# Row loads by head parity, 64x64 transposes, and V of the first batch on a second DMA queue

## The chip, the cores and the metric

One core of one Trainium2 chip. The metric is device time in microseconds (us), the median of several runs. Fast runs of one kernel mostly agree within about 0.6%. PE is the matmul engine, DVE the vector engine, ACT the engine for activations, POOL and SP the engines that here mostly issue DMAs. The profile books every DMA of this program, from whichever queue, on the same 16 DMA engines. A packet here is one contiguous run of a transfer; its bytes are those that land, so a load that rounds f32 to bf16 counts at half of what it reads.

## The reference, cut to what matters

```python
# q, k, v: (8 batches, 8 heads, 576 tokens, 64), float32
scores = q @ k^T / 8 - slope[h] * |i - j|,  masked to 0 <= i - j < 128
attn   = softmax(scores)
x      = (attn @ v) as (8 * 576 tokens, 512)
h      = x @ w_in                       # 512 -> 2048
out    = (h * cos(h)) @ w_out           # 2048 -> 512
```

Almost all the work is in the two last products. Attention of batch c+1 is interleaved with the products of the 512-token chunk c. The first batch has nothing to hide behind.

## The kernel before: the parts that matter

The kernel collects operations with the tiles that they read and write, orders them with a small list scheduler, and emits them with semaphores. POOL's operations keep the order of the program text.

```python
def load_qk(which, src, b, pl):          # batches 0 and 1: rows on partitions
    fns = []
    for g in range(2):                   # two DMAs of 64 partitions, f32 -> bf16 on the way
        fns.append(... qB[which][64*g:64*g+64, 2*pl:2*pl+2, :] <- heads 4g+2pl, 4g+2pl+1 ...)
    op("pool", fns, ...)

def load_v(b, order=range(NBLK)):        # five tiles of 128 (the last 64) tokens x 8 heads x 64
    for t in order:                      # f32 -> bf16 on the way: packets of 64 elements
        op("pool", [vp[b%2][0:rows, t, :, 0:64] <- v[b, :, 128*t:..., :]], ...)

def load_w_in(u): ...                    # 4 loads on POOL's queue, packets of 512 elements

# ---- order of the program (POOL keeps it) ----
for pl in range(2):
    load_qk("q", q, 0, pl); load_qk("k", k, 0, pl)
    if pl == 0:
        constants()                      # masks' input, identity: on POOL
load_v(0)
masks()                                  # 8 exponentials of 128x512 on ACT
... transposes of q and k of batch 0 (PE, 18 of 128x128 per half) ...
for u in range(4): load_w_in(u)
... q, k of batch 1; w_out; V of batch 1 ...
attention(0)
```

P*V of the first half of the tokens needs V tiles 0 and 1, that of the second half tiles 1 to 3, that of the last 64 tokens tiles 3 and 4.

The softmax here doesn't subtract the row's maximum and nothing guards it: scores larger than these inputs give would overflow.

## Time and profile before

| | before |
|---|---|
| time, median of 5 runs | 330.28 us (329.52 to 330.59) |
| first scores / first P*V / first P*V of the last 64 tokens ("tail") / first output matmul | 10.69 / 15.01 / 29.63 / 43.29 us |
| last k of batch 0 landed | 12.32 us |

From the page of the profile: the span, the engines' busy times, PE's busy tenths in 40 slices of the span, the clock row, and the chain of work that ended last, by engine.

```profile
span 328.4 us, 6317 instructions
PE 311.0 (95%) x2504; PEld 161.5 (49%) x2544; DVE 197.9 (60%) x440; ACT 212.6 (65%) x313; POOL 101.3 (31%) x133
...
PE   2589999999999999999999999999999999999995
...
PEclk9999999999999999999999999999999999999999
...
PE 89%; DVE 3%; ACT 2%; POOL 2%; issue 2%; DMA 1%; POOLq 0%; ACTq 0%
```

PE is the limit everywhere except in the first two or three slices of 8.2 us. A change to the first batch's loads can move only that stretch. The clock row does not show what the matmuls' durations show: up to about 24 us PE runs at half rate (128x256 matmuls start 0.21 us apart, later 0.11). The trace's clock records begin with full rate at 24.2 us, and the row shows full rate before the first record as well.

The chain of waits of the first 30 us, its part just before the first P*V (start, duration, what):

```profile
5.83 1.17 POOL qrows L311 x2
7.00 0.54 POOL krows L311
7.54 4.78 DMA krows<-in_k_dram
...
12.36 1.19 PE ps L419 x17
...
13.58 0.82 DVE kt L431
14.40 0.48 DVE p L515
...
15.01 0.32 PE ps L550 x3
```

The second pair of row loads is issued only at 5.83 us, after POOL has built the constants. Its k is waited for until 12.32. Then come its transposes, its eviction on DVE, the first masking behind it in DVE's order, and P*V.

How V and w_in reach the core in this stretch (DMA view, 8 to 16 us; the last column is the median time from issue to landing):

```profile
w_inb<-in_moe_w_in_dram POOLq DMA_DIRECT2D x4, 512.0 KB, 9.5
vp<-in_v_dram POOLq DMA_DIRECT2D x4, 128.0 KB, 5.2
```

What two queues do to each other, while an output store on SP's queue met loads on POOL's (DMA view, 52.5 to 53 us):

```profile
q1 hardware_dynamic: 78, 0.16, 93.3%
q0 software_dynamic: 83, 0.01, 31.7%
```

78 store packets of 2 KB and 83 load packets of 128 B started in that half microsecond. That is nearly one to one, equal turns, although one packet was sixteen times the other.

### The profile page before, as it was taken

What the parts mean: (1) busy time and instruction counts of PE and PEld (TensorE: products, weight loads), DVE (VectorE), ACT (ScalarE), POOL (GpSimd) and SP (SyncE); (2) the same over time, 40 slices, a digit from 0 to 9 for tenths busy, and PEclk for the clock granted to TensorE, in tenths of its full rate; (3) what the DMA queues carried; (4) which work ended last, traced back from release to release, by engine and by line L of the source; (5) the groups of instructions that cost most, each with busy time, mean ns of one, the idle gap of its engine ahead of it and who ended that gap; (6) DMA issues with size and microseconds to landing.
All of it is one profiled execution on the core that took longest, in us unless ns stands there. A gap on an engine that the chain in (4) does not pass through costs nothing.

```text
span 328.4 us, 6317 instructions
## 1 busy us (share of the span) xinstructions
PE 311.0 (95%) x2504; PEld 161.5 (49%) x2544; DVE 197.9 (60%) x440; ACT 212.6 (65%) x313; POOL 101.3 (31%) x133
## 2 busy tenths in 40 slices
PE   2589999999999999999999999999999999999995
PEld 2367755444544454445444644554455444444442
DVE  2569858585848683969586867576567361254000
ACT  5669768686868585867785788669767663263211
POOL 8999530194572726800780050000000000000000
PEclk9999999999999999999999999999999999999999
DMA  6999999999999999991999395100010000201112
GB/s 89 160 206 204 207 157 177 156 150 151 183 158 153 208 115 162 171 92 52 156 168 105 72 152 39 66 33 2 32 64 2 34 1 32 93 5 64 66 67 93
DMA packets 133918, 35.29 MB, mean 107 GB/s; under 512 B 123136, under 2 KB 129280, under 8 KB 133888
## 3 DMA queue, kind: packets, MB, share of 16 engines
q0 software_dynamic: 100288, 18.36, 70.7%
q1 hardware_dynamic: 33600, 16.52, 21.9%
q8 instruction: 20, 0.33, 0.4%
q14 instruction: 10, 0.08, 0.1%
HBM read 36.70 MB, written 9.44 MB: 141 GB/s over the span
## 4 chain that ended last, share of the span: by engine, by line
PE 89%; DVE 3%; ACT 2%; POOL 2%; issue 2%; DMA 1%; POOLq 0%; ACTq 0%
PE ps L688 37%; PE ps L642 33%; PE ps L665 5%; PE ps L470 5%; PE ps L550 3%; PE ps L614 2%; PE ps L553 2%; DMA krows<-in_k_dram 1%; PE ps L419 1%; DVE p L515 1%; ACT p L500 1%; PE ps L460 1%; POOL qrows L311 1%; PE ps L536 1%; PE ps L538 1%
## 5 line engine op out<-in xcount | busy, mean ns | idle before, releaser
L688 PE MATMUL ps<-w_outb,gT 128*128 128x512 bf16 x548 | 133.4, 379 | 1.9 <-issue 0.6
L642 PE MATMUL ps<-xT,w_inb 128*128 128x512 bf16 x500 | 117.9, 379 | 1.2 <-DVE gT L651 0.4
L651 DVE TENSOR_TENSOR gT<-ps,cos 128x512 bf16<-128x512 f32 x128 | 81.8, 686 | 46.8 <-PE ps L688 29.0
L647 ACT ACTIVATE cos<-ps,halfpi 128x512 f32<-128x512 f32 x128 | 81.8, 689 | 23.0 <-PE ps L688 11.9
L688 PEld LDWEIGHTS ps<-w_outb,gT 128*128 128x128 bf16 x576 | 53.6, 98 | 57.9 <-issue 2.2
L500 ACT ACTIVATE p<-ps 128x768 bf16<-128x768 f32 (+1 forms) x64 | 56.1, 915 | 29.3 <-PE ps L470 29.2
L642 PEld LDWEIGHTS ps<-xT,w_inb 128*128 128x128 bf16 x512 | 46.8, 98 | 55.8 <-DVE gT L651 4.8
L320 POOL DMA_DIRECT2D vp<-in_v_dram x40 | 34.0, 907 | 54.2 <-PE ps L553 46.9
L515 DVE TENSOR_TENSOR p<-p,emask 128x768 bf16<-128x768 bf16 (+1 forms) x64 | 39.1, 613 | 0.2
L694 ACT ACTIVATE ob<-ps 128x512 f32<-128x512 f32 x24 | 14.3, 597 | 33.8 <-PE ps L688 33.8
L330 POOL DMA_DIRECT2D qnat<-in_q_dram x30 | 25.5, 920 | 30.9 <-DMA qt<-qnat 30.9
L330 POOL DMA_DIRECT2D knat<-in_k_dram x30 | 25.6, 926 | 5.4 <-DMA kt<-knat 5.0
L584 DVE TENSOR_TENSOR xnat<-ps,rec 128x256 bf16<-128x256 f32 x64 | 26.6, 418 | 0.7
L628 ACT ACTIVATE xT<-ps 128x256 bf16<-128x256 bf16 (+3 forms) x41 | 14.5, 355 | 18.0 <-PE ps L614 17.9
L550 PE MATMUL ps<-vp,p 128*128 128x65 bf16 x256 | 23.0, 199 | 1.6 <-DVE p L515 1.6
L550 PEld LDWEIGHTS ps<-vp,p 128*128 128x128 bf16 x256 | 17.5, 100 | 11.2 <-issue 4.2
L553 PE MATMUL ps<-vp,p 128*128 128x65 bf16 x192 | 20.7, 197 | 0.0
L470 PE MATMUL ps<-qt,kt 64*128 64x128 bf16 (+1 forms) x320 | 20.6, 253 | 0.0
L696 DVE COPY ob<-ps 128x512 f32<-128x512 f32 x12 | 8.3, 690 | 18.4 <-PE ps L688 18.0
L614 PE MATMUL ps<-ident,xnat 128*128 128x128 bf16 x128 | 18.4, 227 | 0.5 <-DVE xnat L584 0.5
L582 DVE RECIPROCAL rec<-ps 128x4 f32<-128x4 f32 x64 | 11.5, 180 | 11.5 <-PE ps L553 10.4
L665 PE MATMUL ps<-xT,w_inb 128*128 128x256 bf16 x128 | 17.4, 281 | 0.7 <-ACT ptail L492 0.5
(52 smaller groups left out, 201.9 us busy)
## 6 DMA issues: line engine op xcount, KB each, us to landing
out_dram<-ob SPq DMA_DIRECT2D x36, 256.0 KB, 2.0
vp<-in_v_dram POOLq DMA_DIRECT2D x32, 128.0 KB, 8.2
qnat<-in_q_dram POOLq DMA_DIRECT2D x24, 128.0 KB, 6.0
knat<-in_k_dram POOLq DMA_DIRECT2D x24, 128.0 KB, 5.8
w_inb<-in_moe_w_in_dram POOLq DMA_DIRECT2D x4, 512.0 KB, 9.5
w_outb<-in_moe_w_out_dram POOLq DMA_DIRECT2D x4, 512.0 KB, 17.8
qrows<-in_q_dram POOLq DMA_DIRECT2D x8, 144.0 KB, 7.4
krows<-in_k_dram POOLq DMA_DIRECT2D x8, 144.0 KB, 8.2
```

The costliest lines, as they stand in the source:

```text
L320: op("pool", [lambda e, t=t, rows=rows: e.dma_start(vp[b % 2][0:rows, t, :, 0:64], v[b, :, 128 * t:128 * t + rows, :].rearrange("h p d -> ...
L330: fns.append(lambda e, t=t, rows=rows: e.dma_start(nat[which][0:rows, t, :, :], src[b, :, 128 * t:128 * t + rows, :].rearrange("h p d -> p ...
L470: ins = e.matmul(ps[:, banks[x], c0:c1], keys_ap(b, x, pr, kc), query_ap(b, x, pr, qb, 128 * nb), start=True, stop=True)
L500: op("act", lambda e: e.activation(P[i][:, :, lo:512], src_[:, :, lo:512], ACTF.Exp, scale=0.125), w=held + [("P", i)], occ=920 if u[1] el ...
L515: op("dve", lambda e: e.tensor_tensor(P[i][:, :, lo:512], P[i][:, :, lo:512], EM[:, 2 * pr:2 * pr + 2, lo:512], ALU.mult), r=[("P", i), (" ...
L550: ins = e.matmul(o, P[i][:, x, d0:d0 + 128], V[:, kc, h, 0:65], start=True, stop=not two)
L553: ins = e.matmul(o, P[i][:, x, p0:p0 + 128], V[:, kc - 1, h, 0:65], start=False, stop=True)
L642: op("pe", lambda e, kc=kc: e.matmul(ps[:, bank, :], w_in[:, kc, 128 * fc:128 * fc + 128], xT[:, kc, r0:r0 + CH], start=(kc == 0), stop=(k ...
L647: op("act", lambda e: e.activation(cosb[ci][:, :], ps[:, bank, :], ACTF.Sin, bias=halfpi[:, 0:1]), r=["halfpi"], w=[("B", bank), ("cos", c ...
L651: op("dve", lambda e: e.tensor_tensor(gT[gi][:, fc, :], ps[:, bank, :], cosb[ci][:, :], ALU.mult), r=[("cos", ci)], w=[("B", bank), ("g", ...
L665: op("pe", lambda e, i=i, fc=fc, kc=kc: e.matmul(ps[:, bank, 256 * i:256 * i + 256], w_in[:, kc, 128 * fc:128 * fc + 128], xT[:, kc, r0:r0 ...
L688: op("pe", lambda e, t=t, fc=fc, bank=bank: e.matmul(ps[:, bank, :], gT[gi][:, fc, 128 * t:128 * t + 128], w_out[:, fc, :], start=(fc == 0 ...
```

## The change

The intent: bring q and k in with one DMA per two head pairs and all four loads before the constants; halve the mask exponentials; transpose in 64x64 tiles that fit the new layout; and free POOL's queue of V of batch 0 by sending it, unrounded, over SP's queue, so that w_in can follow k at once on POOL's. POOL then rounds V to bf16.

```diff
 def load_qk(which, src, b, pl):
-    two DMAs of 64 partitions, heads 4g+2pl, 4g+2pl+1
+    op("pool", [lambda e: e.dma_start(
+        qB[which][:, 2 * pl:2 * pl + 2, :],
+        src[b, 4 * pl:4 * pl + 4, :, :].rearrange("(k x) (s j) d -> (x s) k (j d)", x=2, j=9))], ...)
+
+def load_v0():                           # vst lies in gT[1], which is still free
+    for t in range(NBLK):
+        op("sp", [lambda e, t=t, rows=rows: e.dma_start(vst[0:rows, t, :]..., v[0, :, 128*t:..., :]...)],
+           r=[("qB", "k", 0 if t < 2 else 1)], w=[("vst", t)], ...)   # waits for k to land
+def round_v0():
+    for t in range(NBLK):
+        op("pool", tensor_copy vp[0][0:rows, t, :, 0:64] <- vst, r=[("vst", t), ...], w=[("v", 0, t)], ...)
 ...
 masks:  8 exponentials of 128x512 on ACT  ->  8 of 128x256, and 4 copies on DVE
 transposes: 18 of 128x128  ->  36 of 64x64 per half
 units of batch 0: pairs 0, 2, 1, 3  ->  0, 1, 2, 3
 scheduler: one DMA wire in its model  ->  one per issuing engine
 ...
 for pl in range(2):
     load_qk("q", q, 0, pl)
     load_qk("k", k, 0, pl)
-    if pl == 0:
-        constants()
-load_v(0)
+constants()                              # identity first
+load_v0()
 masks()
 ...
 for u in range(4):
     load_w_in(u)
+round_v0()
```

More of the change, by code (lines that the diff above doesn't have):

```diff
@@ L89, in schedule @@
         free = {e: 0 for e in ENG}
-        wire = self.WIRE0
+        wire = {e: self.WIRE0 for e in ENG}
         mode, table = 0, None
@@ L140, in schedule @@
             if o.dma is not None:
-                wire = max(wire, st + 2300) + o.lat
-                o.end = max(wire, st + o.occ + 1400) + 500
+                wire[e] = max(wire[e], st + 2300) + o.lat
+                o.end = max(wire[e], st + o.occ + 1400) + 500
             else:
@@ L281, in bass_alibi_sliding__then__act_gcu_kernel @@
         dif = sb("dif", [128, 2, 128], F32)
+        vst = gT[1][:, :, :].rearrange("p a b -> p (a b)").bitcast(F32)[:, 0:2560].rearrange(
+            "p (t f) -> p t f", t=NBLK)
         ps = ctx.enter_context(nc.psum_tensor("ps", [128, 8, 512], F32))
@@ L308, in load_qk @@
         def load_qk(which, src, b, pl):
-            fns = []
-            for g in range(2):
-                fns.append(lambda e, g=g: e.dma_start(
-                    qB[which][64 * g:64 * g + 64, 2 * pl:2 * pl + 2, :],
-                    src[b, 4 * g + 2 * pl:4 * g + 2 * pl + 2, :, :].rearrange(
-                        "h (s j) d -> s h (j d)", j=9)))
-            op("pool", fns, w=[("qB", which, pl)], dma=f"ld{which}{pl}", occ=1250, lat=1450)
+            op("pool", [lambda e: e.dma_start(
+                qB[which][:, 2 * pl:2 * pl + 2, :],
+                src[b, 4 * pl:4 * pl + 4, :, :].rearrange("(k x) (s j) d -> (x s) k (j d)",
+                                                          x=2, j=9))],
+               w=[("qB", which, pl)], dma=f"ld{which}{pl}", occ=700, lat=1450)
+        def load_v0():
+            for t in range(NBLK):
+                rows = 128 if t < 4 else 64
+                op("sp", [lambda e, t=t, rows=rows: e.dma_start(
+                    vst[0:rows, t, :].rearrange("p (h d) -> p h d", h=H),
+                    v[0, :, 128 * t:128 * t + rows, :].rearrange("h p d -> p h d"))],
+                   r=[("qB", "k", 0 if t < 2 else 1)], w=[("vst", t)], dma=f"ldf{t}",
+                   occ=350, lat=8 * rows)
+        def round_v0():
+            for t in range(NBLK):
+                rows = 128 if t < 4 else 64
+                op("pool", lambda e, t=t, rows=rows: e.tensor_copy(
+                    vp[0][0:rows, t, :, 0:64],
+                    vst[0:rows, t, :].rearrange("p (h d) -> p h d", h=H)),
+                   r=[("vst", t), ("vinit", 0)], w=[("v", 0, t)], occ=600, lat=700)
         def load_v(b, order=range(NBLK)):
@@ L363, in constants @@
             sel = ["sel"]
+            op("pool", lambda e: e.memset(ident[:, :], 1.0), w=["ident"] + sel)
+            op("pool", lambda e: e.affine_select(
+                ident[:, :], ident[:, :], pattern=[[1, 128]], compare_op=ALU.is_equal,
+                fill=0.0, base=0, channel_multiplier=-1), r=["ident"], w=["ident"] + sel, occ=350)
             op("pool", lambda e: e.iota(dif[:, :, :], pattern=[[128, 2], [-1, 128]], base=-128,
@@ L373, in constants @@
                 fill=-1.0e6, base=0, channel_multiplier=-1), r=["dif"], w=["dif"] + sel, occ=350)
-            op("pool", lambda e: e.memset(ident[:, :], 1.0), w=["ident"] + sel)
-            op("pool", lambda e: e.affine_select(
-                ident[:, :], ident[:, :], pattern=[[1, 128]], compare_op=ALU.is_equal,
-                fill=0.0, base=0, channel_multiplier=-1), r=["ident"], w=["ident"] + sel)
             for i in range(2):
@@ L397, in masks @@
                 op("act", lambda e, h=h: e.activation(
-                    EM[:, h, :].rearrange("p (r f) -> p r f", r=2),
-                    dif[:, :, :].rearrange("p a b -> p (a b)")[:, None, :].broadcast_to([128, 2, 256]),
-                    ACTF.Exp, scale=slopes[h]), r=["dif"], w=[("EM", h)], occ=520, lat=612, table=0)
+                    EM[:, h, 0:256], dif[:, :, :].rearrange("p a b -> p (a b)"),
+                    ACTF.Exp, scale=slopes[h]), r=["dif"], w=[("EM", h)], occ=300, lat=400,
+                   table=0)
+                if h % 2:
+                    op("dve", lambda e, h=h: e.tensor_copy(
+                        EM[:, h - 1:h + 1, 256:512], EM[:, h - 1:h + 1, 0:256]),
+                       r=[("EM", h - 1), ("EM", h)], w=[("EM", h - 1), ("EM", h)],
+                       occ=250, lat=330)
             for x in range(2):
@@ L417, in f @@
                     for j in range(j0, j1):
-                        for x in range(2):
-                            ins = e.transpose(
-                                dst(n)[64 * x:64 * x + 64, 128 * (j - j0):128 * (j - j0) + 128],
-                                qB[which][:, 2 * pl + x, 64 * j:64 * j + 64], ident[:, :])
+                        for k_ in range(2):
+                            for x in range(2):
+                                lo, c0 = slice(64 * x, 64 * x + 64), 128 * (j - j0) + 64 * k_
+                                ins = e.transpose(
+                                    dst(n)[lo, c0:c0 + 64],
+                                    qB[which][lo, 2 * pl + k_, 64 * j:64 * j + 64],
+                                    ident[lo, lo])
                 return ins
@@ L425, in qk_transposes @@
             for n, (j0, j1) in enumerate(jj):
-                o = tr[which][b % 2][:, :].rearrange("p (g l t) -> p g l t", g=2, l=2)[
-                    :, :, pl, 0:576].rearrange("p g (s j) -> p g s j", j=9)[:, :, :, j0:j1]
-                i = dst(n).rearrange("p (j g s) -> p g s j", j=j1 - j0, g=2)
+                o = tr[which][b % 2][:, :].rearrange("p (k t) -> p k t", k=NPAIR)[
+                    :, 2 * pl:2 * pl + 2, 0:576].rearrange("p k (s j) -> p k s j", j=9)[
+                    :, :, :, j0:j1]
+                i = dst(n).rearrange("p (j k s) -> p k s j", j=j1 - j0, k=2)
                 op(("act", "dve"),
@@ L438, in tkeys @@
                 return [("tr", w_, b % 2) for w_ in ("q", "k")] + [("ktail", b % 2)]
-            pls = range(2) if pr is None else [pr % 2]
+            pls = range(2) if pr is None else [pr // 2]
             return [("tr", w_, b % 2, pl, j0) for w_ in ("q", "k") for pl in pls
-                    for j0 in (0, 5)] + [("ktail", b % 2)]
+                    for j0 in (0, 5)] + [("tr", w_, b % 2) for w_ in ("q", "k")] + [
+                        ("ktail", b % 2)]
         def units(b):
             if b == 0:
-                return [(pr, G) for G in range(2) for pr in (0, 2, 1, 3)] + [("t", None)]
+                return [(pr, G) for G in range(2) for pr in range(NPAIR)] + [("t", None)]
             return [("t", None)] + [(pr, G) for pr in range(NPAIR) for G in range(2)]
```

## The prediction

> **What bounds the kernel now.** The page: span 328.4 us, PE busy 311.0 (95%); the chain of waits is 89% PE. By stretches, PE is busy 29.7 of the 30 us from 30 to 60, but 5.4 of the first 15. So only the start can gain.
>
> The start, from the timeline and the chain: POOL issues the first q and k halves from 1.32 to 3.9 us, builds masks and identity (to 5.8), and only then issues the second pair; its k lands at 12.32. Then transposes (1.19), kt eviction on DVE (0.82), the masking behind it in DVE's order (0.48), and the first P*V at 15.01; the second half's starts at 21.5. PE runs at half rate meanwhile: 128x256 matmuls are 0.21 us apart up to 24.1 us, 0.11 after, which the Trainium skill ("TensorE: Matmul & The Clock Gate", Part 1) puts down to an array not yet busy for a whole window.
>
> **What the change does, costed.**
> 1. Row loads: 8 half-loads of batch 0 (0.6-0.8 us of POOL each) become 4, estimated 0.72 each, all out by 4.2 us. At the trace's 150-175 row packets per us (256 per load) they land near 5, 6.7, 8.3 and 10 us, not 12.3. Critical: about 2 us.
> 2. Masks: ACT 0.61 -> about 0.38 each; but their input is ready at about 6.2 instead of 5.2, so the first scores, behind them in ACT's order, still come near 10.5 (10.7 before). Gain near 0.
> 3. Plain pair order: the first mask no longer queues behind the last kt eviction. First P ready near 12.7.
> 4. Transposes: 36 of 64x64 for 18. Warm, 18 took 0.62 us; 16 tail scores of that size took 0.36, so 36 cost an estimated 0.8: over batch 1's four at most +0.8 on PE.
> 5. V of batch 0 leaves POOL's queue (4.3 us of POOL) for SP's; POOL rounds it (estimate 0.7 us a tile). POOL's w_in loads start near 6.2 instead of 12.3, so V, 64 packets of 256 B per engine and tile, shares the engines with k and w_in. The skill ("DMA: Bandwidth & Descriptors", Queues, rings and completion order) says an engine goes round-robin by packet. The trace agrees: while a store met loads (52.5-53 us), 16 packets of each started per 0.1 us. DMA transposes got up to 4 to 1. If V gets one to one, each packet waits for one of 80-94 ns: tile 1 lands near 20 us, first P*V at 21, a loss of 3-4 us. At 4 to 1: 13.6, a gain of 1; at 8 or more, 2.5-3.
>
> **Prediction.** Steps 1 and 3 are worth 2-3 us at the first P*V, step 4 costs under 1, step 5 decides the sign. Weighed: 329.4 us, 8 in 10 between 326.3 and 334.5. Faster by over 2%: 0.03; within 2%: 0.91; slower: 0.06.
>
> **What would show each step.** Right: no DMA gap between 6 and 9.75 us; last k landing at 9-11; first P*V at 12.5-14.5 with PE waiting for DVE; later stages at unchanged distances. Wrong at step 5: PE waiting for POOL's rounding, and POOL for V; first P*V after 16 us; V landing 8 us or more after issue. Step 4: batch 1's four transposes at about 0.8 us instead of 0.62.
>
> **What would make it wrong.** V starved more than one to one; POOL's rounding far over 0.7 us; the clock released sooner or later by more than the start moved; the reordered middle adding PE waits.

## The result, and the profile after

The changed kernel takes 339.3 us (338.79 to 339.86, 5 runs): 1.0277 times before, 95% interval 1.0259 to 1.0296. It is slower. A ratio is the mean of one kernel's fast runs over the mean of the other's fast runs of the same rounds, so it is not quite the ratio of the medians.

The same lines of the page, without the clock row:

```profile
span 337.6 us, 6610 instructions
PE 310.8 (92%) x2648; PEld 162.1 (48%) x2688; DVE 195.6 (58%) x442; ACT 211.5 (63%) x315; POOL 96.4 (29%) x125
...
PE   2508999999999999999999999999999999999996
...
PE 85%; DMA 7%; DVE 3%; ACT 3%; issue 1%; POOL 0%; SPq 0%; ACTq 0%; POOLq 0%
```

PE has the same work (310.8 us busy against 311.0). The loss is idle time in the third and fourth slice. The chain of waits over the first 45 us names it:

```profile
1.32 0.83 POOL qrows L311
2.15 5.54 DMA krows<-in_k_dram
...
7.71 0.44 SPq L321
...
8.21 16.94 DMA gT<-in_v_dram
...
25.20 0.62 POOL vp L330
...
25.86 0.34 PE ps L578 x3
```

Once k has landed (7.69), SP issues V's tile loads, and the second tile is waited for until 25.15. POOL rounds it in 0.62, and only then can the first P*V start, at 25.86 instead of 15.01. From the waits of all engines in the first 30 us (us in total, times, longest):

```profile
POOL vp L330 <- DMA gT<-in_v_dram: 16.3, 4, 10.9
...
PE ps L578 <- POOL vp L330: 10.8, 1, 10.8
```

POOL looks like the culprit on PE's line. Its own line says that POOL waited for the DMA. The DMA view from 6 to 25 us gives the landing times, and that from 12 to 22 us the packets of the two queues (packets, MB, share of the 16 engines):

```profile
w_inb<-in_moe_w_in_dram POOLq DMA_DIRECT2D x4, 512.0 KB, 12.2
gT<-in_v_dram SPq DMA_DIRECT2D x4, 256.0 KB, 13.7
```

```profile
q0 software_dynamic: 1566, 1.55, 91.4%
q1 hardware_dynamic: 1547, 0.39, 29.6%
```

In these 10 us POOL's queue (w_in, packets of 1 KB) sent 1566 packets and SP's queue (V, packets of 256 B) 1547. That is one to one. One pair took 10 us * 16 engines / 1547 = 103 ns per engine, so V's first two tiles, 128 packets per engine (2048 spread over 16), need 13.2 us. On POOL's queue, before, the same V landed 5.2 us after its issue.

Where the 9 us of span went, by stages of the two profiled runs (us):

| stage | before | after | difference |
|---|---|---|---|
| to the first P*V | 15.01 | 25.86 | +10.85 |
| to the first P*V of the tail | 14.62 | 12.13 | -2.49 |
| to the first output matmul | 13.66 | 13.92 | +0.26 |
| to the end | 285.06 | 285.69 | +0.63 |

The timelines show three differences that shorten the second stage. Two masked P tiles and two more exponentials lie ready by then, and PE's idle time falls from 1.39 to 0.47 us. Eight of the stage's score matmuls have already run (40 instead of 48). And half rate lasts 6.6 us of the stage instead of 9.2. The third holds batch 1's four transposes: 0.69 us each instead of 0.62, which makes 0.28.

### The profile page after: what moved, and what is told of

Its sections match the earlier page's. It is cut to its first block, busy times and chain, and to the rows that moved or that the text cites. A ratio compares the mean times of both kernels' runs of the same rounds, so it can differ in the third digit from the quotient of the medians.

```text
span 337.6 us, 6610 instructions
## 1 busy us (share of the span) xinstructions
PE 310.8 (92%) x2648; PEld 162.1 (48%) x2688; DVE 195.6 (58%) x442; ACT 211.5 (63%) x315; POOL 96.4 (29%) x125
## 4 chain that ended last, share of the span: by engine, by line
PE 85%; DMA 7%; DVE 3%; ACT 3%; issue 1%; POOL 0%; SPq 0%; ACTq 0%; POOLq 0%
PE ps L716 35%; PE ps L670 33%; DMA gT<-in_v_dram 5%; PE ps L498 4%; PE ps L693 3%; PE ps L578 3%; PE ps L642 2%; DMA krows<-in_k_dram 2%; PE ps L581 1%; DVE p L543 1%; PE ps L444 1%; PE ps L488 1%; PE ps L564 1%; DVE xnat L612 1%; PE ps L566 1%
## 5 line engine op out<-in xcount | busy, mean ns | idle before, releaser
L338 POOL DMA_DIRECT2D vp<-in_v_dram x35 | 29.7, 892 | 50.0 <-PE ps L581 47.6
L722 ACT ACTIVATE ob<-ps 128x512 f32<-128x512 f32 x29 | 17.3, 596 | 34.5 <-PE ps L716 31.6
L656 ACT ACTIVATE xT<-ps 128x256 bf16<-128x256 bf16 (+3 forms) x38 | 13.4, 353 | 28.6 <-PE ps L642 28.5
L498 PEld LDWEIGHTS ps<-qt,kt 64*128 64x128 bf16 x320 | 11.4, 99 | 9.2 <-issue 3.2
```

Source lines behind the costliest of these rows:

```text
L338: op("pool", [lambda e, t=t, rows=rows: e.dma_start(vp[b % 2][0:rows, t, :, 0:64], v[b, :, 128 * t:128 * t + rows, :].rearrange("h p d -> ...
L498: ins = e.matmul(ps[:, banks[x], c0:c1], keys_ap(b, x, pr, kc), query_ap(b, x, pr, qb, 128 * nb), start=True, stop=True)
```

## The experiments

"Before" below is the kernel before in the same session. Its median was 329.8 to 329.9 us in each of the three sessions. The columns give times in the profiled run. "Full rate" is the time from which PE ran at full rate for good, by the trace's clock records; earlier spells at full rate are in brackets. For "after" and "warm2_v_pool" no record lies in the trace, and the matmuls' durations show it.

| run | median us | ratio to before (95%) | first P*V | tail's P*V | full rate from |
|---|---|---|---|---|---|
| before | 330.28 | 1 | 15.01 | 29.63 | 24.2 |
| after | 339.30 | 1.0277 (1.0259-1.0296) | 25.86 | 37.99 | 32.5 |
| v_pool | 329.43 | 0.9987 (0.9966-1.0007) | 13.03 | 28.58 | 24.3 |
| w_in_held | 332.28 | 1.0081 (1.0060-1.0102) | 14.80 | 28.25 | 27.7 |
| v_alone | 337.65 | 1.0243 (1.0217-1.0269) | 22.02 | 36.67 | 32.9 |
| w_in_small | 338.10 | 1.0262 (1.0237-1.0287) | 22.05 | 36.84 | 34.0 (and 27.1-30.6) |
| v_first | 330.40 | 1.0011 (0.9993-1.0029) | 15.64 | 29.47 | 22.1 (and 15.3-18.7) |
| w_in_after_2 | 329.02 | 0.9977 (0.9960-0.9994) | 15.76 | 28.22 | 22.9 (and 12.7-16.1) |
| v_pool_oldmask | 328.35 (one run) | - | 13.07 | 26.72 | 20.3 |
| warm_before | 329.30 | 0.9989 (0.9969-1.0009) | 14.05 | 29.36 | 23.5 (and 6.4-16.6) |
| warm_v_pool | 328.74 | 0.9971 (0.9947-0.9995) | 13.74 | 27.66 | 22.1 (and 5.0-15.3) |
| warm2_v_pool | 326.79 | 0.9920 (0.9902-0.9939) | 14.67 | 26.94 | before 5.5 |
| v_pool_again | 329.79 | 1.0002 (0.9988-1.0016) | 14.43 | 29.26 | 24.0 (and 13.8-17.2) |

The theory: V starves behind w_in, because each DMA engine gives the two queues one packet each in turn. The rivals: the other parts of the change cost time; SP's queue or POOL's rounding is slow by itself; or the engine shares by bytes, not by packets.

### v_pool: V back on POOL's queue, all else kept

```diff
-        load_v0()
+        load_v(0)                  # after constants(), ahead of w_in
...
-        round_v0()
```

> The changed kernel with V of batch 0 back on POOL's queue (behind q and k, ahead of w_in, no rounding on POOL), all else kept. Theory (V starves one packet to one behind w_in, the rest of the change is sound): V's 4608 packets of 128 B follow k at about 1200 per us, tile 1 is there by 12.5-13, the first P*V comes at 12.8-14 us instead of 25.9, and the time falls to 326.5-329 us, below before. Rival (the row loads, the transposes, the masks or the new order cost time themselves): the first P*V still comes after 16 us, or the time stays above 331 us.

Measured: first P*V at 13.03 us, tail at 28.58, 329.43 us, 0.9987 of before. The first P*V now waits for its masking and not for V (timeline of PE):

```profile
13.03 0.33 PE L578 MATMUL ps<-vp,p 128*128 128x65 bf16 x3 [0.49 <-DVE p L543]
```

The theory's part holds: without the move of V the loss is gone. The total missed its range (326.5 to 329) by 0.4 us at the top, and is not clearly below before: of 2 us won at the first P*V, 1.05 are left at the tail and 0.55 at the end. That became the second question below.

### v_alone: the kernel before with only V moved

```diff
-        load_v(0)
+        load_v0()
...
             load_w_in(u)
+        round_v0()
```

The changed scheduler's wire per engine came along, and one dependence on the transposed tiles that the race check asked for.

> The kernel before with only V moved (SP's queue, POOL's rounding, the scheduler's two wires; one dependence added that the check asks for). Theory: V starves here just as well, because w_in is now issued right behind k: V's packets at about 150 per us, tile 1 near 25 us, first P*V at 25-27 us instead of 15.0, time 338-341 us, so the move alone explains the whole loss. Rival (the loss comes from the combination, or from the other parts): below 334 us.

Measured: 337.65 us, ratio 1.0243, first P*V at 22.02. The move of V alone makes most of the loss. Both numbers fall short of what was expected (338-341, first P*V at 25-27): POOL issues w_in at 8.12 us here instead of 6.35, and its first packet starts at 12.1 us. V's first started at 9.36, so from 10 to 12 us V moved at 350 to 500 packets per us beside the last row loads (61 to 80 per us); with w_in it fell to 70 to 180. Of the expectations only the rival's alternative, below 334 us, is far off.

### w_in_held: POOL rounds V first, and only then issues w_in

```diff
-        for u in range(4):
-            load_w_in(u)
         round_v0()
+        for u in range(4):
+            load_w_in(u)
```

> The changed kernel with POOL's five roundings of V put ahead of its four w_in loads, so that w_in cannot start before V has landed; V stays on SP's queue. Theory (starvation by w_in): V runs at about 1100 packets per us, tile 1 lands by 13-14.5 us, the first P*V at about 14-15 us, w_in lands some 7 us later than in the change, total 328-331 us. Rival (SP's queue is slow by itself for 256 B runs, or rounding on POOL is): V needs as long as in the change (about 150 packets per us), tile 1 lands after 20 us and the time stays near 339 us.

Measured: first P*V at 14.80, as expected. V is not slow on SP's queue when w_in is not loaded beside it, and POOL rounds a full tile in 0.61 to 0.77 us. Both rivals fall. The total, 332.28, missed its range by 1.3 us. The wait had only moved: POOL issues w_in at 17.4 instead of 6.4 us, the first w_in matmul comes at 24.91, and the stage from the tail to the first output matmul grows to 16.31 us (13.66 before), with PE busy throughout: it holds 112 of the w_in matmuls instead of 89. Full rate also came late, at 27.7 us.

The pair also shows a part of the loss that the one-to-one rule does not explain. Packets in the window from 8 to 11 us, in the change and then in this run (DMA view of each):

```profile
q0 software_dynamic: 464, 0.49, 115.7%
```

```profile
q0 software_dynamic: 338, 0.35, 72.6%
q1 hardware_dynamic: 1278, 0.32, 48.1%
```

SP issues V at about 7.7 us in both. With w_in held, 1278 of its packets start before 11 us. With w_in issued from 6.35 us on, none does: the first starts at 11.6, 3.9 us after issue and after w_in's first (9.9), where in the held run it starts at 9.35, 1.6 us after issue. The only difference on the queues is w_in. In v_alone, where V's first packet came ahead of w_in's, it took 1.8 us. How w_in keeps V's first packet back for some 2 us was not settled.

### w_in_small: w_in in packets of half the size

```diff
-            op("pool", [lambda e: e.dma_start(w_in[:, :, 512*u:512*u+512], ...)], ...)
+            op("pool", [lambda e, c=c: e.dma_start(w_in[:, :, c:c+256], ...)
+                        for c in (512*u, 512*u+256)], ...)
```

> The changed kernel with each w_in load cut into two of 256 columns, so that its packets are 512 B instead of 1024 B and twice as many; bytes and order unchanged. Theory (the engine alternates packet by packet): a V packet now waits for a packet of about half the time, V goes at about 250 packets per us instead of 155, tile 1 lands near 19-21 us instead of 25.1, the time falls by 3-5 us to 334-336 us. Rival (the engine shares by bytes or by time): V's rate of bytes stays, tile 1 near 25 us, 338-340 us.

Packets from 12 to 22 us (DMA view):

```profile
q0 software_dynamic: 2430, 1.21, 87.6%
q1 hardware_dynamic: 2420, 0.61, 46.3%
```

This decides between packets and bytes. V went at 242 packets per us instead of 155 and is again equal to w_in's in number, now at half of its bytes instead of a quarter. V's packet itself was not touched. The first P*V came at 22.05 instead of 25.86. Yet the total's median fell by only 1.2 us, against an expected 3 to 5, and the intervals of the two ratios overlap, so that no gain in the total is shown. The chain of waits says why:

```profile
13.35 15.49 DMA gT<-in_v_dram
28.89 0.62 POOL vp L330
29.56 0.20 PE ps L579
```

The second half's P*V now waits until 28.84 us for later tiles of V. w_in has 256 such packets per engine and V 288. At one to one V ends when w_in ends, wherever its first tiles fall. I had counted the first tiles alone.

### v_first: V let go at the start of the program

```diff
-                   r=[("qB", "k", 0 if t < 2 else 1)], w=[("vst", t)], ...
+                   w=[("vst", t)], ...
```

> The changed kernel with V's loads on SP's queue let go at the start of the program instead of after k has landed; w_in still issued early. Theory (one packet of V per packet of whatever POOL's queue holds): V's first packet before 4 us instead of 11.5; V and the 64 row packets per engine of q and k alternate, so one tile lands by 10-11 us and the last k about 1 us later than in the run with V on POOL's queue; after that V is back at about 155 packets per us beside w_in: tile 1 near 17 us, tile 3 not before 24, when w_in is through. First P*V at 17-19 us, second half not before 25, total 334-338 us. Rival (the loss comes from V's late first packet): V complete by 16 us and the total near that of the run with V on POOL's queue, 328-331 us.

Packets from 2 to 4 us, and from 10 to 18 us:

```profile
q1 hardware_dynamic: 1684, 0.43, 93.8%
q0 software_dynamic: 4, 0.00, 1.5%
```

```profile
q0 software_dynamic: 1222, 1.25, 91.5%
q1 hardware_dynamic: 1219, 0.31, 29.1%
```

The total, 330.40 us, lies in the rival's range, and my 334 to 338 was wrong. The rule itself held from 10 to 18 us: 1222 to 1219. It did not hold from 4 to 8 us, beside the row loads alone:

```profile
q0 software_dynamic: 392, 0.43, 78.3%
q1 hardware_dynamic: 999, 0.25, 31.9%
```

There the median packet of V took 18 ns, as from 2 to 4 us with no neighbour, and not 31 as beside w_in. That fits engines on which no row packet was waiting; no run tests it. What I had missed is V's head start. Before q's packets came in number (4 of them by 4 us), V sent 1684 of its 4608, and its first tiles were early enough even with one to one later on. In exchange q and k came late (first transposes at 8.49 instead of 5.52). So here the order in which packets reached the engines decided, and not the queue that they came by.

### w_in_after_2: w_in between the roundings of tiles 1 and 2

```diff
+        round_v0((0, 1))
         for u in range(4):
             load_w_in(u)
-        round_v0()
+        round_v0((2, 3, 4))
```

> The changed kernel with POOL's w_in loads put between the roundings of V's tiles 1 and 2 (in the change: before all five; in the run with w_in held: after all five). Theory (V needs its tiles before w_in's packets are in the rings, and w_in needs to start as early as it may): first P*V at 14.5-15 as with w_in held, w_in's first packet 2-3 us earlier than there (it was 18 us), tiles 2 and 3 no longer starved because most of their packets have gone by then, first w_in matmul near 22 instead of 24.9, total 329.5-331.5 us. Rival (any w_in beside V starves it as in the change): second half of P*V after 26 us, total over 333 us.

Measured: first P*V at 15.76 (expected 14.5 to 15), w_in issued at 15.64 us (17.37 with all of V ahead of it), first w_in matmul at 21.86, 329.02 us and ratio 0.9977, slightly better than its range. By the time w_in's first packet started (17.2), V's last had gone (16.7): there is no overlap left to starve in. That packet came 1.7 us earlier than with w_in held, not 2 to 3. So the change with V on SP's queue does no harm here if w_in is issued once V's first two tiles have landed; held until all of V was rounded, it cost 0.8% (w_in_held). The two runs also differ in when full rate began (22.9 and 27.7 us), so the gap between them is not w_in's wait alone.

### Where v_pool's early start went

v_pool and before reach full PE rate at the same time, 24.3 and 24.2 us. If both leave half rate at the same moment, work that starts earlier gains only half of its head start. That was the theory. The rival was that ACT and DVE bound this stretch. To test it, idle time of PE before the first P*V was filled with matmuls of zeros into a PSUM bank that later work overwrites:

```diff
+        warm(20)                                # at the start
 ...                                             # after q's and k's first transposes:
+                warm((8, 4)[i], [("T", 0, which, 0)])     # (4, 6) in warm_before
```

> The kernel with V on POOL's queue, plus 32 matmuls of zeros into a bank that the scores overwrite, placed in PE's idle time before the first scores (20 at the start, 8 and 4 between the transposes). Theory (the 2 us won at the first P*V shrink to 0.5 because the array runs at half rate until 24.3 us in both kernels): PE goes to full rate before 9 us, transposes take 0.69 instead of 1.17 us, first P*V at 12-13 us, the tail's P*V 2.5-4 us earlier than 28.58, total 325-327 us. Rival (ACT and DVE bound this stretch, not the rate of PE): tail's P*V moves by under 1 us, total 328.5-330 us.

> The kernel before with the same 30 idle-time matmuls of zeros and nothing else. Theory (half rate until 24.2 us costs the start): first P*V about 14.5-15, tail's P*V 2-3.5 us earlier than 29.63, total 326.5-328.5 us; the gap to the run above then shows what the earlier loads are worth at full rate, 1-2 us. Rival: within 0.3% of before.

Both missed their ranges, with 328.74 and 329.30 us where 325-327 and 326.5-328.5 were expected, and both totals lie where the rival had put them. The profile tells why. PE reached full rate at 5.0 (6.4) us, but fell back to half at 15.3 (16.6) us, after the idle stretch before the first P*V, until 22.1 (23.5). The zeros had not reached the stretch in question. A second set closed the gap:

```diff
+        warm(12, [("T", 0, "k", 1)], UB[1])     # until the first P*V
+        warm(5, [("PV", 0, 1)], OB[0], 1)       # after the second
```

> The first run with idle-time matmuls went to full rate at 5.0 us but fell back to half rate from 15.3 to 22.1 us, after the gap of 1.5 us before the first P*V. Here 12 more matmuls of zeros fill that gap and 5 the next. Theory (half rate is what eats the early start): full rate from about 5 us on without a break, tail's P*V at 25-26.8 us (28.58 without, 27.66 with the first set), total 325-327 us. Rival (ACT, DVE and w_in's arrival bound the stretch from 14 to 24 us): full rate throughout, but the tail's P*V still at 27-28 us and the total within 0.3% of the first set.

> The kernel with V on POOL's queue once more, to stand beside the run above on the same chip. Both theories: 0.995-1.001 of before; it tells whether the 0.4 us by which it was faster is real.

The first transposes of k, in v_pool and in warm2_v_pool (timeline of PE: start, duration, operation; the label L is the line):

```profile
8.04 1.17 PE L444 MATMUL ps<-ident,krows 64*64 64x64 bf16 x36 [1.35 <-DMA krows<-in_k_dram]
```

```profile
8.06 0.76 PE L445 MATMUL ps<-ident,krows 64*64 64x64 bf16 x36 [0.80 <-DMA krows<-in_k_dram]
```

Measured: 326.79 us, ratio 0.9920 (0.9902 to 0.9939), against 1.0002 (0.9988 to 1.0016) for v_pool on the same chip. This is the one version that beats both kernels clearly, by 0.8%. In its profiled run, with 327.9 us one of the slower two of six, V even landed late:

```profile
14.67 0.25 PE L579 MATMUL ps<-vp,p 128*128 128x65 bf16 x3 [1.28 <-DMA vp<-in_v_dram]
```

Still the stretch from there to the tail took 12.27 us instead of 15.55 in v_pool and 14.83 in v_pool_again. PE's idle time in it was as in v_pool (1.3 and 1.4 us); its busy time fell from 14.19 to 10.96 us. So the rate of PE, and not ACT or DVE, set most of this stretch. That half rate ate what the earlier loads had won stays argued: the kernel before was not run with this second set, and the first P*V here is only 0.3 us earlier than before's. The tail's P*V, at 26.94, missed its range (25 to 26.8) by a little. v_pool's own gain over before is not established: 0.9987 once, 1.0002 again, and its first P*V at 13.03 and 14.43 in two profiles, because the first k landed at 8.0 and at 9.4 us.

### v_pool_oldmask: the mask exponentials of before

```diff
-    8 exponentials of 128x256 on ACT, 4 copies of 128x2x256 on DVE
+    8 exponentials of 128x512 on ACT
```

> The kernel with V on POOL's queue and the mask exponentials of before (8 of 512 columns on ACT, no DVE copies). One look. If the halved masks were worth nothing, as predicted: first scores and first P*V within 0.4 us of 10.6 and 13.03. If they were worth something: ACT finishes the key eviction 1-2 us later, first scores at 11.5-12.5, first P*V near 14-15.

First scores at 10.66 and first P*V at 13.07, against 10.62 and 13.03. In both profiles the first k landed at 8.0 us, so they can be compared: the halved masks were worth nothing at that point, as predicted. Its tail came earlier (26.72), and in this one execution PE reached full rate at 20.3 us. One run does not say whether that moment is luck.

## Why the prediction was wrong

**The step that failed is step 5, its weighing and its size.** The prediction said that V "shares the engines with k and w_in", quoted the trace for one to one between a store and loads, and then gave weight to a share of 4 to 1 or better, which only DMA transposes had shown. The measured share was 1547 to 1566 packets. The branch that applied was written down ("one to one ... tile 1 lands near 20 us, first P*V at 21, a loss of 3-4 us"), and it was too small as well. These are its terms as measured:

- V's first packet started at 11.6 us, 3.9 us after issue. The prediction implied about 8. With w_in held, it was 1.6 us after issue.
- A pair of packets took 103 ns. The prediction took 80 to 94 for w_in's or k's packet and hardly anything for V's own. Over 128 pairs the difference is one to three us.
- From these two, tile 1 landed at 25.15 us instead of 20.
- Of the delay at the first P*V, the prediction's figures imply that a third to a half is won back later (6 us late, 3-4 us lost). Of 10.85 us, 2.49 came back, and 0.89 was lost again later.

The Trainium skill was read correctly and then not believed enough. The page "DMA: Bandwidth & Descriptors", Queues, rings and completion order, says that an engine takes turns between rows by packet. This agrees, in three places: 1566 to 1547, 2430 to 2420 after halving w_in's packets, 1222 to 1219 beside the row loads and w_in. The stretch of v_first with 999 to 392 is the exception.

**Step 1** (row loads, about 2 us) was right for the first P*V in one profile (13.03) and 0.6 us in another (14.43). All four loads were out by 4.3 us, as predicted (4.2). But the last k landed at 11.3 us in the change, 11.0 in v_pool and 12.3 in v_pool_again, not near 10, against 12.3 before. The gain shows in the start and is not established in the total.

**Step 2** (masks, near 0) was right: 10.66 and 10.62 us for the first scores.

**Step 3** (first P ready near 12.7) was right within half a microsecond: the first masking ended at 13.3 us in the change, and lay idle for 12 us.

**Step 4** (transposes, at most +0.8) was right in sign, and smaller: 0.69 instead of 0.62 us each, +0.28 in all. The skill's "TensorEngine Tiling (Array Packing)", Key Properties, says that tiles load weights and multiply in parallel. The trace agrees: batch 1's 64x64 transposes start in pairs 3 ns apart, a pair about every 31 ns. The 18 of before started in such pairs too, one about every 55 ns.

**The clock** was named and not followed up. The skill's "TensorE: Matmul & The Clock Gate", Part 1, says that the array starts at half rate and needs a busy window to leave it. In this kernel that lasts until 20 to 24 us in the runs where neither V nor w_in is late and no zeros are added, with one spell of 3.4 us at full rate in some. What this takes from the gain of earlier loads was argued above, not measured.

So steps 1 to 4 together are v_pool, between 0.9987 and 1.0002 of before. Step 5 alone is v_alone, 1.0243. The change has both and stands at 1.0277; the intervals of these two overlap, so no loss beyond step 5's is shown.

## What to carry to other kernels

A second DMA queue was here a second claim on the same engines, and where both had packets waiting they were served one for one: V's small packets moved at the pace of w_in's large ones (155 per us beside 1 KB, 242 beside 512 B), so what is needed first must reach the engines first. Before a transfer is moved, count its packets per engine, multiply by the time of the neighbour's packet plus its own, and check every deadline, not only the first. And in a start-up stretch ask at which rate PE runs: here filling PE's idle time won 0.8%, and the earlier loads by themselves nothing that is established.

## What the Trainium skill lacked or had wrong

- "DMA: Bandwidth & Descriptors", Queues, rings and completion order: it says that an engine drains a packet of typically 9 to 17 descriptors before it switches. Counted in the profile's packets, each one contiguous run, the queues alternate singly: 1566 to 1547 for runs of 1 KB and 256 B, 2430 to 2420 for 512 B and 256 B. In the change's trace at 15 us the starts repeat every 105 ns, with 15 or 16 packets of each queue in every repeat, as many as there are engines.
- Same page: no statement of what this does to a load of small runs beside one of large runs. Here a full V tile landed 5.2 us after issue (median) in POOL's queue ahead of w_in, and 13.7 beside it.
- Same page, Specifications: about 0.6 us to the first byte for a load from SP's queue. Here the first packet started 1.1 us after the start of the issuing instruction in v_first and w_in_after_2, 1.6 in w_in_held, and 3.9 in the change, with w_in issued ahead of it. Why w_in adds so much is open.
- "TensorE: Matmul & The Clock Gate", Part 1: it gives about 4 us of sustained matmuls for the warm-up, and less than 1% of a kernel as its cost. The size agrees (0.8% won). What it lacks is how full a window has to be. In a loosely filled start PE was at half rate until 24 us (before); with zeros added it was at full rate from 5.0 us and fell back at 15.3, after 1.5 us of idle time before the first P*V (warm_v_pool); with that idle time cut to 1.3 us it did not fall back (warm2_v_pool).
- No page says that a profile's clock row can read full where no clock record lies: the row shows nine tenths and more from the first slice, while in the kernel before 128x256 matmuls start 0.21 us apart until 24 us.
